# Token tiles 4 to 7 of a feed-forward layer in joint 512-column units from the seventh column block on instead of the tenth

## The chip, the cores and the metric

The kernel runs on one NeuronCore of one Trainium2 chip. The metric is the device time of one execution in microseconds (us), 204.94 us for the kernel before (median of three runs, 204.71 to 204.94). In the profiles TensorE (PE) multiplies matrices, ScalarE (ACT) applies the GELU, VectorE (DVE) normalises, GpSimd (POOL) helps with small steps, and SyncE (SP) issues most transfers (DMAs).

## The reference

A layer norm of x feeds two branches whose sums are added to x: linear attention (A) and a dense layer with GELU (B). Only B's first product matters here.

```python
xn = _layernorm(x, axis=-1)                  # x: 2048 tokens x 640, bf16
return x + _A_ref(xn, A_wqkv, A_wo) + _B_ref(xn, B_w1, B_b1, B_w2, B_b2)
# in _B_ref:
h = _gelu(jnp.einsum("bsd,df->bsf", x, w1) + b1)     # w1: 640 x 1536
```

## The kernel before

The tokens are 16 tiles of 128. Each tile is normalised by VectorE into `xn_tm`, and transposed into `xnT`, by a DMA for tiles 3 to 15. W1's 1536 columns are 12 blocks of 128 (`JT` is 12). A unit computes one block for one, two or four tiles: five matmuls (640 is 5 x 128) into one bank of PSUM, the memory in which the products are summed, and one GELU.

```python
def h_unit(t0, n, jb):
    b = take(1)
    w = n * P
    tok = slice(t0 * P, t0 * P + w)
    Pl.ins("tensor", [(lambda e, k=k: e.matmul(
        bank(b, 0, w), W1[:, k, jb * P:(jb + 1) * P], xnT[:, k, tok],
        start=(k == 0), stop=(k == DT - 1))) for k in range(DT)],
        reads=[r_W1[jb * P // FW]] + r_xnT[t0:t0 + n], writes=[B_[b]])
    ...                                      # the GELU on ScalarE
```

A unit reads all its tiles, so its first matmul waits for the last of them. TensorE's order is the order of the calls:

```python
units(2, 1, 0, 10)
units(3, 1, 0, 10)
units(2, 2, 10, JT)
for t in range(4, NT):
    ...                                      # VectorE: statistics, normalise tile t
    xnT_dma(t)                               # SyncE: transpose tile t
    if t in (7, 9):
        dma_x({7: 12, 9: 14}[t], 2)          # SyncE: load x of tiles 12, 13 or 14, 15
...
units(4, 2, 0, 9)                            # tiles 4 and 5, blocks 0 to 8
units(6, 2, 0, 9)                            # tiles 6 and 7, blocks 0 to 8
units(4, 4, 9, JT)                           # tiles 4 to 7 jointly, blocks 9 to 11
units(8, 4, 0, JT)
units(12, 4, 0, JT)
```

## Time and profile before

| | before |
|---|---|
| profiled span | 203.0 us |
| TensorE busy | 199.1 us (98%) |
| VectorE, ScalarE busy | 61%, 36% |
| weight loads (PEld) busy | 60% |
| TensorE clock granted | 1.00 |

The chain that ended last, in order of time: its rows where tiles 4 to 7 are multiplied; the columns are start, length, what, and how many.

```profile
12.20 18.14 PE ps L375 x215
30.34 0.05 issue
30.39 10.74 PE ps L375 x49
```

Line 375 is the matmul of a unit. The chain goes through it without a stop. The 0.05 us is no pause: the two recorded matmuls around it start 0.325 us apart, which is one step of 0.109 and one of 0.216, so the record of one matmul is missing there.

### The profile page before, as it was taken

How to read it: one execution, taken by the hardware profiler on the slowest of the kernel's cores; microseconds unless marked ns; L12 is line 12 of the kernel's file. 1: busy time of each engine (PE TensorE's matmuls, PEld its weight loads, DVE VectorE, ACT ScalarE, POOL GpSimd, SP SyncE). 2: the span in 40 equal slices, each digit the busy share in tenths (PEclk: the TensorE clock that was granted, in tenths of full speed). 3: DMA queues.
4: the chain of work that ended last, by engine and by line, in shares of the span. 5: the costliest groups of instructions: out<-in, count | busy, mean ns of one | idle time of the engine just before them, and what ended most of it. 6: DMA issues, size and time to landing. Idle time of an engine off the chain costs nothing.

```text
span 203.0 us, 3442 instructions
## 1 busy us (share of the span) xinstructions
PE 199.1 (98%) x1317; PEld 121.8 (60%) x1329; DVE 123.0 (61%) x238; ACT 72.8 (36%) x139; POOL 14.4 (7%) x43
## 2 busy tenths in 40 slices
PE   7999999999999999999999999999999999999996
PEld 2799884444457777777756565444444444447775
DVE  4789682000006888999468899896793385356322
ACT  3589886666666544211143596100000000000000
POOL 3145443000000000000000000000000000000000
DMA  5975985999800000000289435115551966084402
GB/s 174 360 259 114 149 181 110 351 275 294 188 0 3 0 0 3 0 0 3 43 273 322 77 66 108 39 29 125 110 116 39 207 106 129 27 196 93 161 32 65
DMA packets 48134, 24.51 MB, mean 121 GB/s; under 512 B 33702, under 2 KB 48118, under 8 KB 48118
## 3 DMA queue, kind: packets, MB, share of 16 engines
q1 hardware_dynamic: 46094, 23.44, 46.4%
q10 hardware_dynamic: 2024, 0.86, 1.7%
q8 instruction: 10, 0.16, 0.3%
q14 instruction: 6, 0.05, 0.1%
HBM read 12.72 MB, written 2.62 MB: 76 GB/s over the span
## 4 chain that ended last, share of the span: by engine, by line
PE 96%; DVE 1%; DMA 1%; issue 0%; DVEq 0%
PE ps L748 27%; PE ps L375 25%; PE ps L524 11%; PE ps L557 11%; PE ps L569 11%; PE ps L690 7%; PE ps L726 2%; PE ps L407 1%; DMA xPK<-in_A_x_dram 1%; DVE stats L331 1%; PE ps L583 1%; PE ps L601 1%; PE ps L396 0%; DVE xn_tm L389 0%; DVE out_l L729 0%
## 5 line engine op out<-in xcount | busy, mean ns | idle before, releaser
L375 PE MATMUL ps<-xnT,W 128*128 128x256 bf16 (+2 forms) x372 | 50.2, 296 | 0.2
L375 PEld LDWEIGHTS ps<-xnT,W 128*128 128x128 bf16 x375 | 32.4, 98 | 17.3
L379 ACT ACTIVATE HG<-ps,b1c 128x256 bf16<-128x256 f32 (+2 forms) x75 | 37.3, 522 | 13.1 <-PE ps L375 11.3
L748 PE MATMUL ps<-HG,W 128*128 128x512 bf16 x177 | 39.2, 379 | 0.2
L748 PEld LDWEIGHTS ps<-HG,W 128*128 128x128 bf16 x180 | 17.6, 98 | 21.2
L569 PE MATMUL ps<-xnT,Wqkv 128*128 128x512 bf16 x96 | 22.2, 379 | 0.2
L524 PE MATMUL ps<-Wqkv,xnT 128*128 128x320 bf16 x160 | 21.9, 299 | 0.0
L557 PE MATMUL ps<-xPK,xn_tm 128*128 128x320 bf16 x160 | 21.9, 299 | 0.0
L524 PEld LDWEIGHTS ps<-Wqkv,xnT 128*128 128x128 bf16 x160 | 15.7, 98 | 6.2
L557 PEld LDWEIGHTS ps<-xPK,xn_tm 128*128 128x128 bf16 x160 | 15.7, 98 | 6.1
L754 DVE SCALAR_TENSOR_TENSOR W<-ps,b2c,xnT 128x512 bf16<-128x512 f32 x15 | 11.3, 751 | 8.9 <-PE ps L748 8.8
L748 PE MATMUL ps<-PQ,Msb 128*128 128x512 bf16 x73 | 16.4, 379 | 0.1
L569 PEld LDWEIGHTS ps<-xnT,Wqkv 128*128 128x128 bf16 x100 | 11.3, 118 | 8.5
L331 DVE BATCH_NORM_STATS2 stats<-xPK 128x6 f32<-128x320 bf16 x32 | 13.7, 468 | 4.4 <-DMA xPK<-in_A_x_dram 4.4
L508 ACT ACTIVATE xn_tm<-ps 128x512 bf16<-128x512 f32 x20 | 11.9, 597 | 9.4 <-PE ps L569 8.7
L511 DVE SCALAR_TENSOR_TENSOR PQ<-ps,xn_tm 128x512 bf16<-128x512 f32 x20 | 13.8, 692 | 2.1
L508 ACT ACTIVATE ek<-ps 128x640 bf16<-128x640 f32 x16 | 11.2, 703 | 9.2 <-PE ps L524 9.2
L511 DVE SCALAR_TENSOR_TENSOR xPK<-ps,ek 128x640 bf16<-128x640 f32 x16 | 13.2, 825 | 1.7
L516 DVE CAST b2c<-out_l 128x5 f32<-128x5 bf16 x1 | 0.2, 172 | 22.4 <-DMA out_l<-b2bc 22.4
L748 PEld LDWEIGHTS ps<-PQ,Msb 128*128 128x128 bf16 x75 | 7.3, 98 | 8.8
L618 DVE SCALAR_TENSOR_TENSOR xn_tm<-PQ,z_sb,xn_tm 128x512 f32<-128x512 bf16 x16 | 12.0, 750 | 0.4
L544 DVE TENSOR_TENSOR Msb<-Msb,xPK 128x640 f32<-128x640 f32 x14 | 11.6, 826 | 0.5
(64 smaller groups left out, 136.1 us busy)
## 6 DMA issues: line engine op xcount, KB each, us to landing
xPK<-in_A_x_dram SPq DMA_DIRECT2D x5, 640.0 KB, 6.9
Wqkv<-in_A_wqkv_dram SPq DMA_DIRECT2D x3, 800.0 KB, 7.0
W<-in_B_w_dram SPq DMA_DIRECT2D x1, 1920.0 KB, 14.8
out_dram<-xPK SPq DMA_DIRECT2D x3, 640.0 KB, 3.6
W<-in_B_w_dram SPq DMA_DIRECT2D x2, 640.0 KB, 6.7
xPK<-in_A_x_dram SPq DMA_DIRECT2D x4, 320.0 KB, 5.9
Wo<-in_A_wo_dram SPq DMA_DIRECT2D x1, 750.0 KB, 11.6
xPK<-in_A_x_dram SPq DMA_DIRECT2D x4, 160.0 KB, 4.4
```

The costliest lines, as they stand in the source:

```text
L331: Pl.ins(v, lambda e: e.bn_stats(stats[:, s, 6 * h:6 * h + 6], x_in[:, t, h * HW:(h + 1) * HW]), reads=[r_x[t]], writes=[r_stats[s][h]])
L375: Pl.ins("tensor", [(lambda e, k=k: e.matmul(bank(b, 0, w), W1[:, k, jb * P:(jb + 1) * P], xnT[:, k, tok], start=(k == 0), stop=(k == DT - ...
L379: Pl.ins("scalar", lambda e: e.activation(HG[:, jb, tok], bank(b, 0, w), ACT.Gelu_apprx_tanh, bias=b1c[:, jb:jb + 1]), reads=[B_[b], r_b1c ...
L508: Pl.ins("scalar", lambda e: e.activation(e2, src, ACT.Exp), reads=br, writes=[re])
L511: Pl.ins(v, lambda e: e.scalar_tensor_tensor(out=d2, in0=src, scalar=0.0, in1=e2, op0=ALU.max, op1=ALU.add), reads=br + [re], writes=[res_ ...
L524: fns.append(lambda e, k=k, h=h, b=b, t=t: e.matmul(bank(b + h, 0, HW), xnT[:, k, t * P:(t + 1) * P], Wqkv[:, k, D + h * HW:D + (h + 1) * ...
L544: Pl.ins(v, lambda e, t=t: e.tensor_tensor(out=zsum, in0=zsum, in1=PK[:, t, :], op=ALU.add), reads=[r_PK[t], r_zsum], writes=[r_zsum])
L557: Pl.ins("tensor", [(lambda e, t=t, h=h, b=b, f=f: e.matmul(bank(b + h, 0, HW), xn_tm[:, t, f * P:(f + 1) * P], PK[:, t, h * HW:(h + 1) * ...
L569: Pl.ins("tensor", [(lambda e, k=k, j=j, b=b: e.matmul(bank(b), Wqkv[:, k, j:D:DT], xnT[:, k, cc], start=(k == 0), stop=(k == DT - 1))) fo ...
L618: Pl.ins(v, lambda e: e.scalar_tensor_tensor(out=yv[c % 2], in0=pq, scalar=z_sb[:, j:j + 1], in1=yv[c % 2], op0=ALU.mult, op1=ALU.add), re ...
L690: return lambda e: e.matmul(bank(b + h, 0, HW), l, r[:, h * HW:(h + 1) * HW], start=(i == 0), stop=(i == JT + DT - 1))
L748: Pl.ins("tensor", lambda e, l=l, r=r, i=i: e.matmul(bank(b), l, r, start=(i == 0), stop=(i == JT + DT - 1)), reads=rd, writes=[B_[b]], ma ...
```

## The change

The intent was fewer and longer instructions: six units of 256 columns become three of 512. The side effect is that tiles 6 and 7 are asked for three units earlier.

```diff
         run_masks(len(mask_jobs))
-        units(4, 2, 0, 9)
-        units(6, 2, 0, 9)
-        units(4, 4, 9, JT)
+        units(4, 2, 0, 6)
+        units(6, 2, 0, 6)
+        units(4, 4, 6, JT)
         units(8, 4, 0, JT)
         units(12, 4, 0, JT)
```

## The prediction

> **What bounds the kernel now.** I read the page first: busy shares, then the chain that ended last. Then the waits of TensorE, the groups by shape, and the timeline around the place that the diff touches.
>
> ```profile
> PE 96%; DVE 1%; DMA 1%; issue 0%; DVEq 0%
> ```
>
> This is the chain by engine. TensorE's matmul stream is the kernel: 96% of the span is matmul after matmul. Of the waits of TensorE, the table lists one, before the first matmul:
>
> ```profile
> PE ps L318 <- DVE warm L288: 1.3, 1, 1.3
> ```
>
> So from then on TensorE never stands still for a transfer or another engine for long enough to be listed. The kernel's time is therefore the sum of start-to-start steps of the matmuls, and anything that makes TensorE wait in the middle adds its whole length to the end, since the in-order stream behind it has no gap to absorb it.
>
> Two groups, by shape, are what the change trades:
>
> ```profile
> L375 PE MATMUL ps<-xnT,W 128*128 128x512 bf16 x132 | 29.0, 379 | 0.2
> ...
> L379 ACT ACTIVATE HG<-ps,b1c 128x512 bf16<-128x512 f32 x27 | 18.5, 687 | 10.8 <-PE ps L375 10.8
> ...
> L375 PE MATMUL ps<-xnT,W 128*128 128x256 bf16 x140 | 15.8, 273 | 0.0
> ...
> L379 ACT ACTIVATE HG<-ps,b1c 128x256 bf16<-128x256 f32 x28 | 13.3, 473 | 2.3 <-PE ps L375 0.5
> ```
>
> The means (379, 273 ns) are latencies of overlapping matmuls, not their pace. The pace comes from two stretches of the timeline, the second of which begins inside the 512-column part:
>
> ```profile
> 20.35 9.99 PE L375 MATMUL ps<-xnT,W 128*128 128x256 bf16 x90
> ```
>
> ```profile
> 30.82 10.31 PE L375 MATMUL ps<-xnT,W 128*128 128x512 bf16 x47
> ```
>
> Columns are start, length, engine, line, operation and count. The last matmul's latency taken off, a step is (9.99 - 0.273)/89 = 0.1092 us for 256 columns and (10.31 - 0.379)/46 = 0.2159 us for 512. The 90 matmuls of the first row are exactly the 18 units of five that the diff shortens: tiles 4 and 5 for column blocks 0 to 8, then tiles 6 and 7 for the same.
>
> ScalarE is no bound here. A 256-column GELU takes 0.473 us against 5 x 0.1092 = 0.546 us of matmuls, and a 512-column one 0.687 against 5 x 0.2159 = 1.079 us.
>
> **What the Trainium skill says.** "TensorE: Matmul & The Clock Gate", section "Back-to-back issue gap", gives N/2.4 + 2.5 ns for a warm matmul: 109.2 ns at 256 columns and 215.8 at 512. The trace agrees with both to 0.1 ns (109.2 and 215.9). So joining two 256-column matmuls saves only the fixed part, about 2.5 ns.
>
> "Perfetto Trace Analysis", section "DMA Instruction — HWDGE (DVE, Sync)", says that a DMA's row in a profile leaves out the movement of the data. The trace agrees: the transposes that fill xnT have rows of 1.2 us and land 2.5 us or more after their start. The landing has to be read from the DMA view.
>
> "Runtime: NRT & Kernel Launch", section "Instruction fetch mechanics", says that an engine's instructions are refilled in 16 KiB blocks of 256 by a DMA queue of its own. The trace shows such transfers on queue q8, of 16384 bytes each, some 226 to 288 TensorE instructions apart. This matters below.
>
> **The change, part by part.** The jobs of column blocks 6, 7 and 8 for tiles 4 to 7 are done as three units of 512 columns in place of six of 256. Set against the kernel before, the instruction order shows 30 matmuls of 256 columns (with 30 weight loads and 6 GELUs) removed, 15 of 512 (with 15 weight loads and 3 GELUs) added, and VectorE, GpSimd and the DMA queue untouched.
>
> First term, throughput: removed 30 x 0.1092 = 3.276 us, added 15 x 0.2159 = 3.238 us. TensorE gains 0.04 us. The 15 weight loads saved (0.098 us each) lie beside matmuls that are longer than they are, and ScalarE's saving of 6 x 0.473 - 3 x 0.687 = 0.78 us is on an engine with slack. Both are worth nothing.
>
> Second term, when tiles 6 and 7 are first needed. Tiles 4 and 5 start at 20.35 us, the start of the row above. Before, nine units of five come first, so tiles 6 and 7 are needed at 20.35 + 45 x 0.1092 = 25.26 us. After, only six come first: 20.35 + 30 x 0.1092 = 23.63 us. The need moves 1.64 us earlier, while their arrival is set by VectorE's normalisations and the transposes, which do not depend on TensorE here. When do they arrive?
>
> ```profile
> 16.81 1.20 SPq L448 DMA_TRANSPOSE xnT<-xn_tm  x1
> ```
>
> ```profile
> 19.45 1.20 SPq L448 DMA_TRANSPOSE xnT<-xn_tm  x1
> ```
>
> ```profile
> q8 instruction: 1, 0.02, 28.8%
> ...
> xnT<-xn_tm SPq DMA_TRANSPOSE x1, 4.9
> ```
>
> The transposes run one tile after the other from tile 3 on; the first fence is tile 5's issue, the second tile 7's, and between them is tile 6's at 18.13. Tile 5 landed 2.5 us after its issue and tile 6, by its own semaphore, at 20.70. The third fence is the DMA view of 20.2 to 20.5 us: an instruction block of TensorE on q8, and the one transpose being issued then, tile 7's, which took 4.9 us. It landed at 24.34. Single packets that began at 21.1 to 21.4 us all ended at 22.7, some 1.5 us each in place of 18 ns: held up behind the instruction block, as I read it.
>
> So before, tile 7 has 25.26 - 24.34 = 0.92 us to spare. After, TensorE arrives at 23.63 and waits 24.34 - 23.63 = 0.71 us. To this comes the restart. The chain at the kernel's start shows TensorE resuming on a semaphore:
>
> ```profile
> 5.06 0.36 DVE xn_tm L389
> 5.42 0.05 issue
> 5.46 0.28 PE ps L396 x2
> ```
>
> That is 0.05 us from signal to start; I add an estimated 0.05 us for refilling the pipeline behind the first weight load. The wait is then 0.71 + 0.10 = 0.81 us.
>
> Nothing behind it is short of data. The joint units read the same four tiles. Tiles 8 to 11 land by 29.99 us and are needed from about 33.4 us; Wqkv's second third and all later inputs land long before their use, and TensorE is not listed as waiting anywhere. So the wait passes whole to the end. Sum: -0.04 + 0.81 = +0.77 us, 204.94 + 0.77 = 205.7 us.
>
> **The rivals.** (a) No wait at all. All undisturbed transposes landed 2.5 to 2.7 us after issue; tile 7 would then land near 22.1 us, 1.5 us before it is needed, and only the throughput term is left: 204.9 us. For it: the 4.9 us are one sample, and the blocking needs a fetch to coincide with the packets. Against it: the fetch is tied to TensorE's place in its program, which is the same up to 23.6 us in both kernels, and the DMA and VectorE work there is the same too, so the coincidence should recur. Tile 15's transpose, issued at 32.49 with a q8 block at 34.99, took 4.5 us, so the effect is not a single accident.
>
> (b) A real gain from fewer, longer matmuls: fewer weight loads, fewer GELUs. For it: weight loads are busy 0.9 of each microsecond in the 256-column part. Against it: the measured step there is already the column time plus the fixed 2.5 ns, so weight loads hide. It would need 4.1 us for 2%, more than all of the 3.28 us removed. At most 204.9 us.
>
> (c) The pause makes TensorE's clock drop. The same TensorE page, Part 1, says that an idle window of about 3.4 us returns the clock to half. For it: the trace has no pause of this kind in mid-kernel to look at. Against it: 0.8 us is a quarter of that window. If it fell, matmuls of up to 3.4 us would take twice as long, and the time would be about 209 us. I give this 1%.
>
> (d) The wait moves: tile 7's landing may come up to half a microsecond earlier or later as the DMA traffic shifts from run to run, giving 205.2 to 206.2 us.
>
> **Range and chances.** The centre leans a little to rival (a): with some 80% for a wait of 0.4 to 1.3 us and 15% for none, the middle is 205.6 us. The range of 204.7 to 206.3 us has room for both below, and for a landing half a microsecond late above. A change of 2% is 4.1 us, which only (c) comes near: faster 0.005, same 0.985, slower 0.01.
>
> **What would show it.** In the profile of the changed kernel: TensorE's list of waits has a new entry, on line 375, for the transfer xnT<-xn_tm, of 0.7 to 0.8 us, once; the 512-column row starts near 27.7 us instead of 30.2, and the block of line 375 ends about 0.8 us later, at 60.2 instead of 59.5; every later line keeps its duration and only its start moves. Tile 7's transpose again takes near 4.9 us, with the q8 block beside it near 20.4 us. Groups of line 375: 110 matmuls of 256 columns and some 150 of 512, at unchanged means. A time of 204.9 us or less with no such wait proves the second term wrong; a clock below 1.00 after 24 us speaks for (c).

## The result, and the profile after

The changed kernel took 206.59 us (median of six runs, 205.60 to 207.50), the one before in the same rounds 204.92 us (six runs, 204.71 to 205.18). The ratio is 1.0082, interval 1.0053 to 1.0111. Ratios are the mean time of one kernel's runs over that of the other's in the same rounds, so not quite the ratio of the medians. Executions over 1.5% slower than the fastest of the same kernel are left out of the means. All runs were at a clock of 1.00. The change costs 1.7 us where 0.77 was predicted, and the time lies above the range.

The chain of the changed kernel, same view:

```profile
12.49 11.59 PE ps L375 x155
24.08 1.46 issue
25.54 35.81 PE ps L375 x180
```

There is one hole. Behind it, 180 matmuls (30 of 256 columns, 150 of 512) run without a stop. The hole ends exactly at the first unit of tiles 6 and 7: the row before it in the timeline is the 30 matmuls of tiles 4 and 5.

```profile
20.64 3.44 PE L375 MATMUL ps<-xnT,W 128*128 128x256 bf16 x30
```

TensorE would have gone on at 20.64 + 30 x 0.1092 = 23.92 us; it went on at 25.54. The wait is 1.62 us. (The chain shows 1.46 because it counts the latency of the last matmul as work.)

TensorE's list of waits has the entry, but under another name than predicted:

```profile
PE ps L375 <- issue: 1.5, 1, 1.5
```

"Issue" means that the profile found nothing that released TensorE. The landing of tile 7 says what did. Its issue, and the DMA view of 20.9 to 21.1 us:

```profile
19.90 1.20 SPq L448 DMA_TRANSPOSE xnT<-xn_tm  x1
```

```profile
q8 instruction: 1, 0.02, 43.3%
...
xnT<-xn_tm SPq DMA_TRANSPOSE x1, 5.5
```

The transpose was in flight for 5.54 us and landed at 25.45; TensorE started 0.09 us later. The block of TensorE's instructions on q8 is beside it, as before.

The rest of line 375 stayed as it was. Its shapes, answering to those shown of before:

```profile
L375 PE MATMUL ps<-xnT,W 128*128 128x512 bf16 x150 | 32.5, 379 | 0.0
...
L375 PE MATMUL ps<-xnT,W 128*128 128x256 bf16 x110 | 12.7, 272 | 1.5 <-issue 1.5
```

From the last matmul of line 375 to the end of the span both kernels take 143.95 us, and so do, to 0.01 us, one more trace of the kernel before and three more of the changed one that follow: what is lost ahead of that point is never won back. From TensorE's start on tiles 4 and 5 to that matmul the kernel before takes 38.75 us and the changed one 40.33: +1.58 us, which is the wait of 1.62 less the 0.04 saved. The rest of the difference between the two spans, 0.29 us, is that TensorE came to tiles 4 and 5 at 20.64 us instead of 20.35. That start lies in code both kernels share. It varied from 20.35 to 21.40 us over the traces, and in the two traces of the kernel before the time follows it (204.41 us with a start at 20.35, 205.54 with one at 21.40). That it is also why the untraced runs of the kernel before reach from 204.42 to 206.31 us was not shown. Where traces are compared below, I use the stretch from that start on.

### The profile page after: what moved, and what is told of

Its sections match the earlier page's. It is cut to its first block, busy times and chain, and to the rows that moved or that the text cites.

```text
span 204.9 us, 3420 instructions
## 1 busy us (share of the span) xinstructions
PE 200.4 (98%) x1314; PEld 120.5 (59%) x1314; DVE 122.7 (60%) x238; ACT 72.0 (35%) x136; POOL 14.4 (7%) x43
## 4 chain that ended last, share of the span: by engine, by line
PE 98%; issue 1%; DVE 0%
PE ps L748 27%; PE ps L375 24%; PE ps L557 11%; PE ps L524 11%; PE ps L569 11%; PE ps L690 7%; PE ps L726 2%; PE ps L318 2%; PE ps L407 1%; PE ps L583 1%; PE ps L601 1%; PE ps L396 0%; DVE out_l L729 0%; DVE warm L288 0%; PE ps L359 0%
## 5 line engine op out<-in xcount | busy, mean ns | idle before, releaser
L375 PE MATMUL ps<-xnT,W 128*128 128x512 bf16 (+2 forms) x360 | 50.5, 302 | 1.5 <-issue 1.5
L375 PEld LDWEIGHTS ps<-xnT,W 128*128 128x128 bf16 x360 | 30.9, 98 | 20.4 <-issue 1.7
L379 ACT ACTIVATE HG<-ps,b1c 128x512 bf16<-128x512 f32 (+2 forms) x72 | 36.5, 533 | 15.5 <-PE ps L375 14.2
L569 PE MATMUL ps<-xnT,Wqkv 128*128 128x512 bf16 x100 | 22.8, 379 | 0.0
```

The lines of the kernel that those rows point to most:

```text
L375: Pl.ins("tensor", [(lambda e, k=k: e.matmul(bank(b, 0, w), W1[:, k, jb * P:(jb + 1) * P], xnT[:, k, tok], start=(k == 0), stop=(k == DT - ...
L379: Pl.ins("scalar", lambda e: e.activation(HG[:, jb, tok], bank(b, 0, w), ACT.Gelu_apprx_tanh, bias=b1c[:, jb:jb + 1]), reads=[B_[b], r_b1c ...
L569: Pl.ins("tensor", [(lambda e, k=k, j=j, b=b: e.matmul(bank(b), Wqkv[:, k, j:D:DT], xnT[:, k, cc], start=(k == 0), stop=(k == DT - 1))) fo ...
```

## The experiments

Theory A: TensorE waits for tile 7's transpose to land, whose landing does not depend on TensorE's need for it, and which is late because a block of TensorE's instructions is fetched while its packets move. Rival B: the load of x behind that transpose makes it late. Rival C: the wait is TensorE lacking its own instructions, as the word "issue" suggests. Rival D: the joint units cost more than their pace shows. "Wait" below is always the step across the hole less one matmul's 0.109 us.

### The number of separate blocks: eight, five, seven

```diff
-        units(4, 2, 0, 6)
-        units(6, 2, 0, 6)
-        units(4, 4, 6, JT)
+        units(4, 2, 0, 8)                    # 5, 7 in the other two
+        units(6, 2, 0, 8)
+        units(4, 4, 8, JT)
```

> Joint units from the ninth block on (eight separate blocks instead of six): TensorE then asks for tiles 6 and 7 some 2 x 0.546 = 1.09 us later than in the changed kernel. Theory A (TensorE waits for tile 7's transpose to land, at a time that does not depend on TensorE): the wait shrinks by 1.09 us from a mean of about 1.7 us to about 0.6 us, so 205.5 us, with a wait at the first unit of tiles 6 and 7. Rival C (the wait marked 'issue' is TensorE lacking its own instructions at that place in the program): the wait stays near 1.6 us and the time near 206.6 us. Rival D (joint units of 512 columns cost more than the matmul pace shows): cost falls with the number of joint units, from three to one, so about 205.5 us too, but without a wait in the trace.

Measured: 205.56 us (205.25 to 206.64), ratio 1.0033 (1.0004 to 1.0062). The trace has no wait: tile 7 landed 3.96 us after the start on tiles 4 and 5 and was needed 4.37 us after it. The chain shows no hole:

```profile
12.92 47.26 PE ps L375 x345
```

So the median equals theory A's number, but in the traced run, itself 205.57 us, it does not come from theory A's wait: TensorE came late to tiles 4 and 5 (21.07 us), and the last output transfer took 2.02 us instead of the 1.45 of the kernel before. That agreement is luck.

> Joint units from the sixth block on (five separate blocks): TensorE asks for tiles 6 and 7 0.546 us earlier than in the changed kernel. Theory A: the wait grows by 0.55 us and nothing else changes, about 207.1 us, wait about 2.2 us. Rival C: about 206.6 us, wait unchanged. Rival D: a third more joint units added to the three, so 206.6 + 1.7/3 = 207.2 us without a longer wait.

Measured: 208.23 us (206.41 to 209.34), ratio 1.0136 (1.0089 to 1.0183). The wait in the trace is 2.23 us, as theory A says. But the runs split in two. Three at a clock of 1.00 took 206.41, 207.12 and 207.68 us, on average 207.07. Three at a mean clock of 0.992 took 208.78 to 209.34. The trace is one of the latter. Its table by stretches, with the granted clock (PEclk) after POOL's busy time:

```profile
25.00:26.50 1.50, 0.47 (x5) 0.45 (x6) 0.00 (x0) 0.00 (x0) 0.48 (x1) 1.00 1.27 215
...
26.90:30.10 3.20, 3.20 (x17) 2.28 (x16) 2.63 (x8) 1.63 (x4) 1.46 (x4) 0.50 0.89 190
...
30.40:32.00 1.60, 1.60 (x10) 0.76 (x9) 1.60 (x6) 0.76 (x2) 0.62 (x2) 1.00 0.82 147
```

After the pause (0.8 us after TensorE went on at 26.04 us) the clock is at half for about 3.4 us: the 3.2 us shown and parts of the two short rows on either side. That costs half of it, 1.7 us: 0.8% of the span, the whole of the missing 0.008. My rival (c) exists, one step beyond this change, at half the cost that I had reckoned for it (3.4 us).

> Joint units from the eighth block on (seven separate blocks). Theory A: TensorE asks for tiles 6 and 7 0.546 us later than in the changed kernel, so with a landing as late as there the wait is about 1.0 us (206.0 us), with one as early as in the kernel before about 0.3 us (205.3 us). Rival C: 206.5 us.

Measured: 206.08 us (205.49 to 206.82, four runs), ratio 1.0055 (0.9997 to 1.0113), wait in the trace 1.06 us with tile 7's transpose in flight for 5.51 us: the first of the two cases expected. The wait goes 2.23, 1.62, 1.06 with five, six and seven blocks, as the need moves later by 0.546 us per block, and is gone with eight. (These three traces are of the late kind described below and that of eight is of the early kind; a late one would leave some 0.5 us.) Rival C, for which it would stay the same, falls. So does D: a joint unit without a wait (split8) costs nothing in the trace, its stretch being 38.74 us against 38.75.

### Tile 7 transposed by TensorE

```diff
-            xnT_dma(t)
+            if t != 7:
+                xnT_dma(t)
+            else:
+                units(4, 2, 0, 4)
+                b7 = transp(7)
+                units(4, 2, 4, 6)
+            if t == 9:
+                xnT_copy(7, b7)
...
-        units(4, 2, 0, 6)
```

> The changed kernel with tile 7 alone transposed by TensorE (five transposes after the fourth unit of tiles 4 and 5, some 0.3 us) and copied by VectorE, instead of by a DMA. Theory A: the wait vanishes, and the time is that of the kernel before plus the transposes, 204.9 - 0.04 + 0.3 = about 205.2 us, with little spread. Rival C: still about 206.5 us or more, as TensorE's program is as long or longer. Rival D: about 206.9 us (three joint units remain).

Measured: 205.22 us (204.94 to 206.22), ratio 1.0014 (0.9985 to 1.0042). The hole is gone, and the five transposes stand in the chain:

```profile
12.77 10.58 PE ps L375 x145
23.35 0.28 PE ps L359 x5
23.63 36.74 PE ps L375 x190
```

The stretch is 38.99 us, 0.24 more than before: 0.28 for the transposes less 0.04. This is theory A's number. With the DMA of this one tile out of the way, the wait is gone. The three joint units cost nothing here, so rival D falls for them too.

### The load behind tile 7

```diff
-            if t in (7, 9):
-                dma_x({7: 12, 9: 14}[t], 2)
+            if t in (8, 9):
+                dma_x({8: 12, 9: 14}[t], 2)
```

> The changed kernel with the load of tiles 12 and 13 of x issued behind tile 8's transpose instead of behind tile 7's. Rival B (the load right behind tile 7's transpose is what makes it late): tile 7 lands about 2.6 us after its issue, the wait vanishes, about 204.9 us. Theory A in its first form (the instruction block alone makes it late): landing again about 5 us after issue, about 206.6 us. A mixture, as the last completion writes of tile 7 in the trace come only among the packets of that load: landing some 3.7 to 4.3 us after issue, wait 0.2 to 0.8 us, about 205.4 us.

Measured: 206.35 us (205.93 to 207.04), ratio 1.0065 (1.0038 to 1.0092). Tile 7 was in flight for 5.53 us and the wait was 1.64 us, with the first packet of the load only just before the landing. Rival B falls, and the mixture that I had thought likely with it.

### The instruction block moved

```diff
-        filler(6)
+        filler(5)
         b1_step()
-        filler(3)
+        small(44)
...
+        def small(n):
+            b = take(1)
+            Pl.ins("tensor", [lambda e: e.matmul(bank(b, 0, 64)[0:32, :], warm[:, 0:32], warm[:, 0:64], start=True, stop=True)
+                              for _ in range(n)], reads=[r_warm], writes=[B_[b]])
```

> The changed kernel, with four of the nine large warm-up matmuls replaced by 44 small ones, so that TensorE has 80 instructions more before its real work and crosses each block of its program some 80 x 0.032 = 2.5 us sooner: the block that met tile 7's transpose at 20.98 us now comes near 18.4 us. Theory A (the block delays whichever transpose is moving): tile 5's or tile 6's transpose is in flight for 4.5 to 5.5 us, tile 7's for about 2.6; if it is tile 5's, TensorE waits about 1.5 us at the first unit of tiles 4 and 5 and not at tiles 6 and 7 (about 206.3 us); if it is tile 6's, the wait is under 0.5 us (about 205.2 us). Rival B' (tile 7 is late for a reason of its own place: queue, load behind, VectorE): tile 7 again 5.5 us, wait 1.5 us at tiles 6 and 7, about 206.5 us.

Measured: 205.96 us (205.64 to 206.12, four runs), ratio 1.0043 (1.0000 to 1.0086). The block came at 18.34 us. DMA view of two stretches, 16.3 to 17.4 us (tile 4) and 20.6 to 21.7 us (tile 7):

```profile
xnT<-xn_tm SPq DMA_TRANSPOSE x1, 4.4
```

```profile
q14 instruction: 1, 0.01, 4.5%
...
xnT<-xn_tm SPq DMA_TRANSPOSE x1, 4.0
```

The delay moved with the block, onto tile 4, which in every other trace takes 2.6 us; I had named tile 5 or 6. Tile 5 took 3.5 and tile 6 3.0 us, queued behind it. Tile 7 fell to 4.0, not to 2.6, with a block of another queue, q14, beside it. The wait at tiles 6 and 7 shrank to about 0.16 us, and the stretch to 38.87 us. A second, new wait of 0.26 us stands before the first unit of tiles 4 and 5, which began 0.09 us after tile 5 landed at 21.13 us (line 380 is here the matmul of a unit):

```profile
17.06 4.06 PE ps L380 x60
21.12 0.10 issue
21.22 39.24 PE ps L380 x210
```

The total is 0.8 us above what I expected for a short wait, but that is not in the span: the spans of the four runs average 203.8 us, as do those of the seven runs of the kernel before in the same rounds. The time exceeds the span by 2.10 us on average instead of 1.37. Why it does so with the edited warm-up stays open.

### The two kernels again

> The changed kernel, unedited, for a second trace. Theory A: one wait of 1.4 to 1.7 us at the first unit of tiles 6 and 7, tile 7's transpose in flight for about 5.5 us, an instruction block of TensorE some 1.0 to 1.1 us after that transpose's issue; 206.4 us. If the flight of 5.5 us was an accident of one trace, it is here nearer the 4.9 us of the kernel before and the wait nearer 0.8 us.

Measured: 207.04 us (205.98 to 207.47, four runs), ratio 1.0090. The traced run was the fastest of the four: wait 0.95 us, tile 7 4.84 us in flight.

> The kernel before, unedited, for a second trace. Theory A: tile 7 again in flight for 4.9 us or more with the instruction block beside it, and no wait, as it is needed only about 4.9 us after tiles 4 and 5; 204.9 us. If the delay of tile 7 was an accident, it lands 2.6 us after its issue.

Measured: 205.54 us, one run. The list shows no wait, but only just. The DMA view of 20.75 to 21.8 us shows tile 7's transpose:

```profile
xnT<-xn_tm SPq DMA_TRANSPOSE x1, 5.6
```

It landed 4.86 us after the start on tiles 4 and 5, and is needed after 45 x 0.1092 = 4.91. With the restart that is a wait of 0.04 us, too short for the list. The kernel before lives at the edge.

> The changed kernel, unedited, for a third trace: the landing of tile 7, counted from TensorE's start on tiles 4 and 5, was near 4.0 us in three traces so far and near 4.8 us in the others, so the wait is near 0.9 us or near 1.6 us; and whichever it is, the last of tile 7's completion writes comes 1.1 to 1.2 us before the landing, right after a block of instructions on queue q14 ends.

Measured: 206.78 us; in flight 5.57 us, wait 1.67 us. The last completion write came 1.18 us before the landing, as a q14 block ended.

> The changed kernel, unedited, for a fourth trace: as for the third.

Measured: 205.62 us; in flight 4.94 us, wait 0.84 us. The last completion write came 1.16 us before the landing, again as the q14 blocks ended. The chain:

```profile
12.33 11.59 PE ps L375 x155
23.91 0.68 issue
24.60 35.81 PE ps L375 x180
```

So one and the same kernel has two sizes of hole, and its time follows: 205.62 and 205.98 us with the short one, 206.39 and 206.78 with the long one.

### Four separate blocks

> Joint units from the fifth block on (four separate blocks): TensorE asks for tiles 6 and 7 1.09 us earlier than in the changed kernel, so the wait is 2.0 or 2.7 us. If the longer wait were only added, the time would be near 207.6 us at a clock of 1.00. If, as in half of the runs with five blocks, the pause brings the clock to half for about 3.3 us, 1.65 us more: near 209.2 us at a mean clock of 0.992, and in more than half of the runs.

Measured: 207.20 us (206.13 to 209.45), ratio 1.0103 (1.0062 to 1.0143) over five runs. The trace has a wait of 1.78 us with tile 7 4.87 us in flight. Only one run of six was at 0.992 (209.45 us, slow); the other five average 207.01. So a clock drop does not simply become likelier as the pause grows: three of six with five blocks, one of six with four, none in 12 runs of the changed kernel. My "more than half" was wrong.

## Why the prediction was wrong

**First term, throughput: right.** The counts of shapes are as said (110 and 150), the means unchanged, and where no wait stands in the trace the joint units leave the stretch as it was. The prediction's citation for the pace (the Trainium skill, "TensorE: Matmul & The Clock Gate", section "Back-to-back issue gap") left out that the section gives its formula for an isolated matmul, and about 131 ns for 512 columns in a stream with weight loads. The stream here ran at 215.9 ns: the formula held, the lower figure did not.

**Second term, the mechanism: right.** Reducing the separate blocks makes TensorE arrive at tile 7 before its transpose lands, and the wait passes whole to the end. Shown by the holes that shrink block by block, by the tile transposed on TensorE, and by the 143.95 us behind the block.

**The restart: right.** The estimate was 0.10 us from landing to matmul. In each of the eight traces with a hole it was 0.09 us.

**The failed step: the landing.** The prediction took "24.34" us from one trace, 3.99 us after TensorE's start on tiles 4 and 5, and argued that, as TensorE's program and "the DMA and VectorE work there is the same too", it would be the same after. In the changed kernel's trace it was 25.45 - 20.64 = 4.81 us after that start. Of the 0.82 us, 0.16 is that the issue came later against TensorE (0.74 us ahead of the start instead of 0.90) and 0.65 that the flight took 5.54 us instead of 4.89. The remaining 0.01 is rounding. The predicted wait of 0.81 us plus 0.82, less 0.01 for the shorter restart, is the measured 1.62. In the fourth trace of the changed kernel, which landed after 4.03 us, the wait was 0.84 us and the time 205.62: for an early landing the predicted sum holds.

This is not something the change did to the transfer. Over the eleven traces in which tile 7 is transposed by DMA and the warm-up is unedited, the landing has two values, in both kernels:

| | traces | issue against start | flight | landing after start | wait with six blocks |
|---|---|---|---|---|---|
| early | 4 (one of before, one of the changed) | -0.90 to -1.00 | 4.87 to 4.94 | 3.88 to 4.03 | 0.84 |
| late | 6 (one of before, two of the changed) | -0.70 to -0.74 | 5.51 to 5.59 | 4.79 to 4.87 | 1.62 to 1.67 |
| between | 1 (changed) | -0.71 | 4.84 | 4.13 | 0.95 |

The records of single packets show where the difference lies. In all of them, 18 to 21 packets of tile 7 stand still until about 3.3 us after its issue, behind the block on q8 as I read it, and most completion writes follow at once. In the early traces two more blocks of instructions, on q14, start right then, take 0.36 us, and the last completion writes come as they end. In the late ones one q14 block has started already at about 1.8 us and takes 1.7 to 1.9 us, the second takes 1.0, and the last completion writes come as that one ends, 0.6 us later. That the q8 block delays a transpose is supported by the experiment that moved it, though how is open: the block has ended 2.4 to 2.6 us after the issue, about 0.8 us before the standing packets do. The part of q14 is seen in every trace of these two groups but was not tested by an edit, and the trace between does not fit it: its q14 blocks are like the late ones (from 1.76 us, 1.80 and 1.00 us long), yet its last completion write came at 3.75 us, as in the early ones. Why the first q14 block starts early in some executions goes with the phase between the engines in the table; what sets that phase, and whose instructions q14 carries, stays open.

**The rivals and the range.** Rival (a), 15% for no wait, did not come: all four traces of the changed kernel have one. Rival (d) allowed half a microsecond either way; the second value lies 0.8 us up, outside. The range failed because its width was guessed from one sample of a transfer that was itself an anomaly. The median of 206.59 us is slightly more than the late value explains: predicted 205.7 plus 0.8 is 206.5. The four traced runs of the changed kernel lost 1.23 us on average in the stretch, and the eight untraced ones took longer than they did. If those eight were all late, the mean loss would be (4 x 1.23 + 8 x 1.6)/12 = 1.5 us. The spans in the run lists agree with that: those of the 12 runs of the changed kernel average 205.08 us, those of the 29 runs of the kernel before in the later rounds 203.64, which is 1.44 us less. Some 0.17 us more lies outside the span, which the time exceeds by 1.54 us instead of 1.37. That all eight were late, and what the 0.17 us is, was not shown.

**What was predicted of the trace.** The name of the wait was wrong ("issue" instead of the transfer). The joint units were expected near 27.7 us and began at about 28.8, since the wait was twice as long. Of the nine distances between blocks on q8 in the trace before, one is 216 instructions, below the 226 given; nothing rests on it. Rival (c) did not occur in the changed kernel's traces or runs, but did at five blocks.

No version measured here beats the kernel before. The only gain on offer is 0.04 us, and the kernel before already has TensorE busy without a hole.

## What to carry to other kernels

Joining work into wider instructions also moves the moment at which its inputs are first needed; when TensorE has no idle time, compare that moment with the landing of every input before counting the instructions saved. A landing that is late in one trace is a sample of a distribution: take several traces of the kernel before, express the landing against the consumer's own clock, and widen the range by what they show. Margins of a microsecond that look like waste in an order of work may be what covers the slow case.

## What the Trainium skill lacked or had wrong

- "Runtime: NRT & Kernel Launch", section "Instruction fetch mechanics", calls the cost of crossing a 16 KiB block of instructions mostly hidden. Here it coincides with a DMA transpose that needs 4.84 to 5.59 us instead of 2.5 to 2.7, and when 80 more instructions brought the block 2.6 us sooner, tile 4's transpose took 4.4 us instead of 2.6 and tile 7's 4.0. No page says outright that an instruction fetch can hold up a transpose.
- "TensorE: Matmul & The Clock Gate", table "Why this matters for your kernels", asks for no idle gaps above about 3 us. With five separate blocks a pause of 2.2 us was followed by half clock for about 3.4 us, and the mean clock of 0.992 that goes with it appeared in three of six runs; after the pauses of 0.8 to 1.7 us in the four traces of the changed kernel it did not appear.
- No page gives the flight of one small transpose between places of SBUF: of a tile of 128 x 640 bf16, with no block of instructions and no load of x beside it, mostly 2.5 to 2.7 us from issue to landing, of which 1.2 us is the issuing engine's.
- No page warns that a wait for a DMA can be marked "issue": in all eight holes TensorE restarted 0.09 us after tile 7's landing, yet the profile named no transfer for the hole.
